# One conv moved behind the sixth tile, one moved ahead of a second stage, and two loads let loose singly

## The chip, the cores and the metric

The kernel runs on one core of a Trainium2 chip. The metric is the device time of one execution in microseconds (us), the median over several executions. Five engines work side by side and meet only at semaphores: TensorE (PE; its weight loads are shown as PEld), VectorE (DVE), ScalarE (ACT), GpSimd (POOL) and SyncE (SP), which here only issues transfers.

## The reference

The input `x` has 8 sequences of 4160 tokens with 192 channels. First comes a causal depthwise convolution of 7 taps whose weights are shared by the 24 channels of a head and normalised over the taps, then a feed-forward part whose hidden layer is the maximum of three products:

```python
w = exp(weight - max); w = w / sum(w)                 # [8 heads, 7 taps]
y[b, s, h, :] = sum_k w[h, k] * x_pad[b, s + k, h, :] # 33280 tokens in all
h = maximum(maximum(y @ w1, y @ w2), y @ w3)          # [tokens, 768]
out = h @ w_out                                       # [tokens, 192], float32
```

## The kernel before, in words

The 33280 tokens are 65 blocks of 512. Every block goes through the same stages.

**Convolution on TensorE.** The taps stand in a band matrix (`band`), and a matmul of a window of `x` with a slice of it gives convolved tokens. Blocks 0 to 3 use `conv_dense` (160 PE instructions: 80 matmuls of 32 columns and their weight loads). It writes channels by tokens into two PSUM tiles `D`, which ACT and DVE copy to `yd`; `cross` copies the two halves of the middle channels to each other. Blocks from 4 on use `conv` (64 matmuls and 64 loads): the result stands with tokens on the partitions in PSUM tiles `G`, `evac` (one ACT copy, one DVE copy for block 4) takes it to `ys`, `turn` issues two transposing DMAs from `ys` to `yp`, and `double` copies `yp` on POOL so that both halves of the partitions hold what they need.

**First stage, `l1(t, j)`.** For block `t` and hidden tile `j` of six: three pairs of matmuls of 512 columns, one lane on each half of the rows, with weights `w1-w3` (PSUM tile `lp`) and `w2-w3` (`lq`). `top` then makes `r = relu(lp)` on ACT and `h = max(r, lq)` on DVE. There are two buffers of `lp` (pool `psp`) and two of `lq` (pool `psq`), so tile `j+2` needs what ACT and DVE did with tile `j`.

**Second stage, `st2(t, upto)`.** 30 matmuls of 192 columns in each of two lanes give `out = h @ w_out + y @ (w3 @ w_out)`. They accumulate in tiles `po` of the pool `psw` (four buffers, which `D` and `G` also take). `upto` says how far each lane has come. At the half and at the end, `total` lets ACT copy one lane (`a`) and DVE add the other (`o`); both free a `po` buffer.

**Order.** The schedule is written by hand: each engine's queue holds the instructions as the program emits them. A loop over `t` from 2 on interleaves `l1(t, j)` with `st2(t - 1, ...)` and, now and then, a conv of a later block, the casts of `x` to fp16 on POOL (`cast_x`) and loads (`load_x`, on SP's queue). `meet` only empties the list of pending matmuls. Block 2 is the first turn of the loop. In it the kernel before emits: `l1(2, 0)`; the rest of block 0's second stage, `st2(0, (30, 30))`; `st2(1, (5, 5))`; `l1(2, 1)`; `conv_dense(3)` into two buffers of `psw`; then `st2` and `l1` in turn, with `conv(4)` after `l1(2, 3)`. Blocks 7, 8 and 9 are loaded into the fp32 buffers `xf_0`, `xf_1` and `xf_2` that blocks 0, 1 and 2 leave. Before each load, rows 32 to 63 of the buffer have to be set to zero (`zero_x`, by ACT for `xf_0`, by DVE for the others). The two transposing DMAs of `turn(4)` stand on SP between the loads of block 8 and those of block 9.

Of the kernel before, what the change touches and what calls it, by code (L numbers as in the profile page):

```python
# [28 lines left out]
def kernel(  # L29
# [12 lines left out]
    nc = tc.nc  # L42
# [45 lines left out]
    NQ = len(chunks_of[0])  # L88
    TOK = 32
    NR = NBLK // TOK // 2  # L90
# [6 lines left out]
        return rows  # L97

    const = ctx.enter_context(tc.tile_pool(name="const", bufs=1))
    x16p = ctx.enter_context(tc.tile_pool(name="x16p", bufs=2))  # L100
    x16q = ctx.enter_context(tc.tile_pool(name="x16q", bufs=2))
    ysp = ctx.enter_context(tc.tile_pool(name="ysp", bufs=2))
    ydp = ctx.enter_context(tc.tile_pool(name="ydp", bufs=4))
# [24 lines left out]
    def zero_x(t, q0=0, q1=NR, eng=None):  # L128

        if t >= NDENSE:  # L130
            get_x(t)
        xf = xbuf[t]
        if eng is not None:
            eng.memset(xf[TOK:HALF, q0:q1, :], 0.0)
            return
        zero = idle[TOK:HALF, 0:D]
        nc.scalar.copy(out=xf[TOK:HALF, q0:q1, :],
                       in_=bass.AP(tensor=zero.tensor, offset=zero.offset,
                                   ap=[list(zero.ap[0]), [0, q1 - q0], [1, D]]))
# [37 lines left out]
    def place(t):  # L177
        return pairs.get(t, (t, 0, 0))
# [3 lines left out]
    def cast_x(t):  # L182
        if not 0 <= t < NB:
            return
        xf, p0, _ = xin.pop(t)
        t0, u, nu = place(t)
        if u == 0:
            pool = x16q if nu == 4 else x16p
            x16s[t0] = pool.tile([P, NHEAD, 4, nu, 2, GRP], FP16, tag="x16", name=f"x16_{t0}")
        if p0:  # L190
            nc.gpsimd.memset(xf[0:p0, 0, :], 0.0)
        K = HALF + KR
        for r in range(2):
            nc.gpsimd.tensor_copy(out=x16s[t0][0:K, :, :, u, r, :].rearrange("p h j c -> p j h c"),  # L194
                                  in_=xf[0:K, 4 * r:4 * r + 4, :].rearrange("p j (h c) -> p j h c", c=GRP))
# [174 lines left out]
    def conv_dense(t, copies, pools=((None, None),) * 2, order=(0, 1)):  # L370


        yd = dense[t] = ydp.tile([P, NC, NBLK], FP16, tag="yd", name=f"yd_{t}")
        for n in order:
            slots_ = ((0, 1, 2, 3), (4, 5, 4, 5))[n]
            pool, tag = pools[n]
            ps = (pool or psw).tile([P, NBLK], FP32, tag=tag or "w", name=f"D{n}_{t}")
            for (q, b, row_lo, rlen, lo, hi, cc) in chunks_of[t]:
                for v in range(2):
                    for g, s in enumerate(slots_):  # L380
                        h = (32 * s + 31 * v) // GRP
                        nc.tensor.matmul(  # L382
                            ps[32 * g:32 * g + 32, lo:hi],
                            lhsT=xz[t][v][0:rlen, q, 32 * s:32 * s + 32],
                            rhs=band[0:rlen, h, cc:cc + hi - lo],
                            start=(v == 0), stop=(v == 1), tile_position=(0, 32 * g))
            copies[n](out=yd[:, 2 * n, :], in_=ps[:])
# [152 lines left out]
    def st2(t, upto):  # L540

        if t < 0:
            return
        if t not in halves:
            todo = [[], []]
            for s in range(4):
                for i in range(2):
                    row = slice(HALF * i, HALF * (i + 1))  # L550
                    m = [(-1, i)]
                    if s % 2 == i:
                        m.append((-1, 2))
                    hh = [(j, row) for j in range(NJ)]
                    m = hh + m if t == 0 else m + hh
                    todo[i] += [(s, n == 0, n == len(m) - 1, e) for n, e in enumerate(m)]
            if t == 0:

                todo = [[(n, first and n % 2 == 0, last, e)
                         for m in (False, True) for n, first, last, e in lane if (e[0] < 0) == m] for lane in todo]  # L560
            halves[t] = (todo, {}, [0, 0], {})
        todo, ps, at, ends = halves[t]

        def product(i, e):
            s, first, last, (j, c) = todo[i][e]
            b0 = s - s % 2
            row = slice(HALF * i, HALF * (i + 1))
            if (b0, i) not in ps:
                ps[b0, i] = psw.tile([P, 2, D], FP32, tag="w", name=f"po{i}_{t}_{s}")
            if j < 0:  # L570
                a, b = y_tok(t, i, c, s), m16[row, c // 2, :]
            else:
                assert done[t] > j
                a, b = hs[t][row, j, P * s:P * (s + 1)], wo[row, j, :]
            nc.tensor.matmul(ps[b0, i][:, s % 2, :], lhsT=a, rhs=b, start=first,  # L575
                             stop=last and (t > 0 or s % 2 == 1))

        def total(s):
            if t not in outs:
                outs[t] = outp.tile([P, 4, D], FP32, tag="o", name=f"o_{t}")  # L580
            a = tp.tile([P, 2, D], FP32, tag="a", name=f"a_{t}_{s}")
            nc.scalar.copy(out=a[:], in_=ps[s - 1, 0][:])  # L582
            nc.vector.tensor_add(out=outs[t][:, s - 1:s + 1, :], in0=a[:], in1=ps[s - 1, 1][:])  # L583

        while any(at[i] < upto[i] for i in range(2)):
            i = 0 if at[0] < upto[0] and (at[0] <= at[1] or at[1] >= upto[1]) else 1
            e = at[i]
            mm(i, D, lambda i=i, e=e: product(i, e))
            at[i] += 1
            s, _, last, _ = todo[i][e]  # L590
            if last:
                ends[s] = ends.get(s, 0) + 1
                if ends[s] == 2 and s % 2:
                    op(lambda s=s: total(s))
        emit()
# [57 lines left out]
    PQ = ((psp, "p"), (psq, "q"))  # L653
    WW = ((psw, "w"), (psw, "w"))
    WPWQ = ((psw, "w"), (psp, "p"), (psw, "w"), (psq, "q"))
    ACT, DVE = nc.scalar.copy, nc.vector.tensor_copy
# [45 lines left out]
    st2(0, (24, 24))  # L702
    meet()
    zero_x(0, NQ)
    zero_x(2, NQ, NR, nc.vector)
    zero_x(3, NQ, NR, nc.vector)
    load_x(7)
    cast_x(5)
# [20 lines left out]
    for t in range(2, NB):  # L729
        u = convs_at.get(t, NB)  # L730
        late = t > 2 and u < NB
        if t in (3, 4):
            double(t + 1)
        if t > 3:
            for v in range(casts.get(t - 1, 8) + 1, casts[t] + 1):
                cast_x(v)
        l1(t, 0)
        if t == 2:
            st2(0, (30, 30))
        elif t == 3:  # L740
            cast_x(8)
            nc.gpsimd.tensor_copy(out=m16[0:HALF, 2, :], in_=m16[HALF:P, 0, :])
            nc.gpsimd.tensor_copy(out=m16[HALF:P, 2, :], in_=m16[HALF:P, 1, :])
        if t > 3 and not late:
            op(lambda t=t: (store(t - 2, 0, 4, (nc.sync,)),
                            turn(t + 2, (2,)) if place(t + 2)[1:] == (0, 4) else None, load_on(t)))
        else:
            op(lambda t=t: store(t - 2, 0, 4, (nc.sync,)))
        cuts = ROOM if late else EVEN
        st2(t - 1, (cuts[0], cuts[0]))  # L750
        for j in range(1, NJ):
            l1(t, j)
            if late and j == 1:
                st2(t - 1, (cuts[0] + OWN + AHEAD, cuts[0] + OWN))
                meet()
                quad, second = u >= QUADS, u < QUADS or t == u - 3
                conv(u, WPWQ, range(4 * second, 4 * second + 4) if quad else range(NHEAD))
                for i in (0, 2):
                    evac(u, i)
                for i in (1, 3):  # L760
                    evac(u, i, nc.vector.tensor_copy)
                if second:
                    turn(u)
                load_on(t)
            if t == 2 and j == 1:
                meet()
                conv_dense(3, (ACT, DVE))
                zero_x(1, NQ, NR, nc.vector)
                cross(3, GP)
                load_x(8)  # L770
                cast_x(6)
            elif t == 2 and j == 3:
                meet()
                conv(u, WW)
                evac(u, 0)
                evac(u, 1, nc.vector.tensor_copy)
                turn(4)
                load_x(9)
                cast_x(7)
            st2(t - 1, (cuts[j], cuts[j]))  # L780
            if j == 1 and t > 4 and t + 2 in pairs and pairs[t + 2][1] % 2 == 0:
                double(t + 2)
            if t == NB - 1 and j == 3:
                op(lambda: store(NB - 2, 0, 2, (nc.sync,)))
        if t == NB - 1:
            op(lambda: store(NB - 2, 2, 4, (nc.sync,)))
# [29 lines left out]
```

## Time and profile before

| | |
|---|---|
| median of 4 runs | 455.27 us (454.81 to 455.78) |
| the profiled execution | 455.38 us, of which the span is 453.6 us |
| PE, PEld busy | 447.8 and 411.6 us |
| DVE, ACT, POOL busy | 358.7, 319.8 and 203.1 us |
| DMA | 72.03 MB, mean 159 GB/s |

The span begins with the first instruction and ends with the last; 1.8 us of the execution lie around it. Line numbers such as L507 are lines of the kernel before. A row of the timeline gives the start, the time, the engine, the line, the operation and, in brackets, the idle time of the engine before it with what ended it. "issue" stands where the engine waited for nothing that the profile shows. SPq rows are the issues of transfers on SP's queue, not the transfers.

### The profile page before, as it was taken

To read this page: it belongs to the slowest core of one execution; us is meant where nothing else is said; L and a number is where in the kernel's file an instruction comes from. 1 tells how busy PE (TensorE), PEld (TensorE's weight loads), DVE (VectorE), ACT (ScalarE), POOL (GpSimd) and SP (SyncE) were. 2 spreads that over 40 slices of the span, in tenths; PEclk is the share of its full clock that TensorE was granted. 3 is DMA by queue.
4 is the path that set the end of the run, shared out by engine and by line. 5 is a ranking of instruction groups with operands and counts; after the bars stand their busy time and mean duration, and the time that the engine had idled before them with its cause. 6 is when DMAs were issued, how large, how long until landed. Compare 5 with 4: busy or idle time off the path is not lost.

```text
span 453.6 us, 18554 instructions
## 1 busy us (share of the span) xinstructions
PE 447.8 (99%) x7730; PEld 411.6 (91%) x7730; DVE 358.7 (79%) x616; ACT 319.8 (70%) x605; POOL 203.1 (45%) x228
## 2 busy tenths in 40 slices
PE   8989999999999999999999999999999999999997
PEld 4468999999999999999999998899999999999996
DVE  7777787878888787888878778887878778787775
ACT  7767777767777677777767777777767777676664
POOL 2684926557453524635244454435346452505000
PEclk9999999999999999999999999999999999999999
DMA  7978997596985759687495949858596865734223
GB/s 204 218 186 148 219 178 218 147 207 167 159 198 140 172 132 180 160 174 195 115 194 135 215 111 178 191 130 189 128 173 162 186 178 117 122 86 106 59 72 106
DMA packets 127987, 72.03 MB, mean 159 GB/s; under 512 B 52064, under 2 KB 127711, under 8 KB 127903
## 3 DMA queue, kind: packets, MB, share of 16 engines
q1 hardware_dynamic: 127743, 70.75, 68.7%
q8 instruction: 60, 0.98, 1.0%
q14 instruction: 24, 0.20, 0.2%
q10 hardware_dynamic: 160, 0.10, 0.1%
HBM read 33.28 MB, written 25.56 MB: 130 GB/s over the span
## 4 chain that ended last, share of the span: by engine, by line
PE 95%; SPq 2%; DMA 1%; issue 0%; POOL 0%; DVE 0%; ACT 0%; POOLq 0%; DVEq 0%
PE po L575 36%; PE lq L507 31%; PE lp L507 22%; PE G L361 3%; DMA ws<-in_moe_w_dram 1%; PE lw L530 1%; SPq L227 1%; SPq L223 1%; PE D L382 0%; PE po L606 0%; PE lp L530 0%; SPq L164 0%; DVE h L495 0%; PE pm L341 0%; POOL xz L211 0%
## 5 line engine op out<-in xcount | busy, mean ns | idle before, releaser
L575 PE MATMUL po<-wo,h 64*128 64x192 f16 x3072 | 333.5, 243 | 0.0
L495 DVE TENSOR_TENSOR h<-r,lq 128x512 f16<-128x512 f16 x384 | 263.0, 686 | 85.4 <-ACT r L494 76.5
L494 ACT ACTIVATE r<-lp 128x512 f16<-128x512 f32 x384 | 229.0, 597 | 115.3 <-PE lp L507 100.9
L507 PE MATMUL lp<-yp,wd 64*128 64x512 f16 x1098 | 295.7, 376 | 0.0
L507 PE MATMUL lq<-yp,wd 64*128 64x512 f16 x1098 | 295.5, 376 | 0.0
L575 PEld LDWEIGHTS <-h 64*128 64x128 f16 x3072 | 243.0, 94 | 6.5 <-issue 4.3
L507 PEld LDWEIGHTS <-wd 64*128 64x128 f16 x2268 | 178.8, 94 | 12.2
L194 POOL CAST x<-xf 103x768 f16<-103x768 f32 x122 | 97.4, 827 | 110.6 <-DMA xf<-in_x_dram 87.9
L575 PE MATMUL po<-m,yp 64*128 64x192 f16 x720 | 141.0, 243 | 0.0
L424 POOL COPY yp<-yp 64x1536 f16<-64x1536 f16 (+1 forms) x62 | 89.6, 1445 | 90.7 <-DMA yp<-ys 82.7
L583 DVE TENSOR_TENSOR o<-a,po 128x384 f32<-128x384 f32 x128 | 70.0, 547 | 0.0
L575 PEld LDWEIGHTS <-yp 64*128 64x128 f16 x720 | 66.3, 94 | 0.4
L582 ACT COPY a<-po 128x384 f32<-128x384 f32 x128 | 60.4, 473 | 0.0
L401 ACT CAST ys<-G 128x384 f16<-128x384 f32 x61 | 26.3, 482 | 10.2 <-PE G L361 9.9
L401 DVE CAST ys<-G 128x384 f16<-128x384 f32 x61 | 31.0, 550 | 0.0
L361 PE MATMUL G<-x,band 39*32 39x192 f16 (+2 forms) x1152 | 17.5, 234 | 0.5 <-issue 0.5
L361 PEld LDWEIGHTS <-band 39*32 39x32 f16 x1152 | 10.7, 91 | 5.8 <-issue 5.3
L507 PE MATMUL lp<-yd,wd 64*128 64x512 f16 x36 | 9.7, 376 | 0.0
L507 PE MATMUL lq<-yd,wd 64*128 64x512 f16 x36 | 9.7, 376 | 0.0
L211 POOL CAST xz<-xf 112x160 f16<-112x160 f32 (+2 forms) x15 | 4.3, 335 | 9.6 <-DMA xf<-in_x_dram 8.1
L530 PEld LDWEIGHTS <-wd 128*128 128x128 f16 (+1 forms) x48 | 3.1, 98 | 6.0 <-issue 2.3
L382 PEld LDWEIGHTS <-xz 112*32 112x32 f16 x320 | 4.9, 108 | 2.9 <-POOL xz L211 1.2
(65 smaller groups left out, 94.7 us busy)
## 6 DMA issues: line engine op xcount, KB each, us to landing
xf<-in_x_dram SPq DMA_DIRECT2D x113, 234.0 KB
out_dram<-o SPq DMA_DIRECT2D x62, 384.0 KB
xf<-in_x_dram SPq DMA_DIRECT2D x7, 204.8 KB
xf<-in_x_dram SPq DMA_DIRECT2D x3, 420.0 KB
ws<-in_moe_w_dram SPq DMA_DIRECT2D x8, 128.0 KB
yp<-ys SPq DMA_TRANSPOSE x62
out_dram<-o SPq DMA_DIRECT2D x5, 192.0 KB
wos<-in_moe_w_out_dram SPq DMA_DIRECT2D x1, 576.0 KB
```

The source lines that it names most:

```text
L194: nc.gpsimd.tensor_copy(out=x16s[t0][0:K, :, :, u, r, :].rearrange("p h j c -> p j h c"), in_=xf[0:K, 4 * r:4 * r + 4, :].rearrange("p j ( ...
L361: nc.tensor.matmul(G[2 * (k // per) + i][TOK * j:TOK * (j + 1), k % per, :], lhsT=band[row, h, HALF * i + LAP:HALF * i + KR], rhs=x16s[t0] ...
L382: nc.tensor.matmul(ps[32 * g:32 * g + 32, lo:hi], lhsT=xz[t][v][0:rlen, q, 32 * s:32 * s + 32], rhs=band[0:rlen, h, cc:cc + hi - lo], star ...
L401: copy(out=slots[t][:, i % 2, :, :, GRP * h0:GRP * (h0 + per)].rearrange("p u r (h c) -> p h (u r) c", c=GRP), in_=G[i][:].rearrange("p h ...
L424: nc.gpsimd.tensor_copy(out=yp[HALF * i:HALF * (i + 1), 1, :, :, :, :].rearrange("p i u k n -> p (i u k n)"), in_=yp[HALF * (1 - i):HALF * ...
L494: nc.scalar.activation(out=r[:], in_=ps[0][:], func=AF.Relu)
L495: nc.vector.tensor_max(out=hs[t][:, j, :], in0=r[:], in1=ps[1][:])
L507: nc.tensor.matmul(ps[i][:], lhsT=w_of(i, c, j), rhs=y_all(t, i, c), start=(n == 0), stop=(n == NC - 1))
L530: nc.tensor.matmul(open_ps[t, j, i][:], lhsT=a, rhs=b, start=(t, j, i) not in begun, stop=(t, j, i) in begun)
L575: nc.tensor.matmul(ps[b0, i][:, s % 2, :], lhsT=a, rhs=b, start=first, stop=last and (t > 0 or s % 2 == 1))
L582: nc.scalar.copy(out=a[:], in_=ps[s - 1, 0][:])
L583: nc.vector.tensor_add(out=outs[t][:, s - 1:s + 1, :], in0=a[:], in1=ps[s - 1, 1][:])
```

## The change

In block 2's turn of the loop, and just ahead of it:

- `st2(1, (5, 5))` no longer stands behind `l1(2, 0)`. Its ten matmuls join the next ones, so that `st2(1, (10, 10))` comes as twenty behind `conv_dense(3)`.
- `conv_dense(3)` takes its two PSUM tiles from the pools of the first stage (`PQ`: one of `psp`, one of `psq`) where it took two of `psw`.
- `conv(4)`, with its copies and its two transposing DMAs, stands behind `l1(2, 5)` where it stood behind `l1(2, 3)`.
- The zeroing of `xf_1` and the loads of block 8 stand behind `l1(2, 2)` where they stood behind `l1(2, 1)`. The zeroing of `xf_2`, which stood ahead of block 2, stands behind `l1(2, 4)`, with the loads of block 9 right behind it. So on SP the loads of block 9 now stand ahead of the two transposing DMAs of `turn(4)`.
- The fp16 pool `x16p` has three buffers in place of two, because block 7 is now cast ahead of `conv(4)` in the program.

Every engine has the same instructions as before (15462 rows on PE, 612 on DVE, 605 on ACT, 137 on POOL, 190 on SP); their order differs.

```diff
-    x16p = ctx.enter_context(tc.tile_pool(name="x16p", bufs=2))
+    x16p = ctx.enter_context(tc.tile_pool(name="x16p", bufs=3))
...
     zero_x(0, NQ)
-    zero_x(2, NQ, NR, nc.vector)
     zero_x(3, NQ, NR, nc.vector)
     load_x(7)
     cast_x(5)
...
         cuts = ROOM if late else EVEN
-        st2(t - 1, (cuts[0], cuts[0]))
+        if t > 2:
+            st2(t - 1, (cuts[0], cuts[0]))
         for j in range(1, NJ):
             l1(t, j)
...
             if t == 2 and j == 1:
                 meet()
-                conv_dense(3, (ACT, DVE))
-                zero_x(1, NQ, NR, nc.vector)
+                conv_dense(3, (ACT, DVE), PQ)
                 cross(3, GP)
-                load_x(8)
                 cast_x(6)
-            elif t == 2 and j == 3:
+            elif t == 2 and j in (2, 4):
+                v = j // 2
+                zero_x(v, NQ, NR, nc.vector)
+                load_x(7 + v)
+                if j == 4:
+                    cast_x(7)
+            elif t == 2 and j == 5:
                 meet()
                 conv(u, WW)
                 evac(u, 0)
                 evac(u, 1, nc.vector.tensor_copy)
                 turn(4)
-                load_x(9)
-                cast_x(7)
             st2(t - 1, (cuts[j], cuts[j]))
```

## The prediction, made before the changed kernel was run

> **What bounds the kernel now.** I read the busy table first, then the chain, the windows of blocks 2, 3 and 4, and the timelines of PE, DVE, SP and POOL there.
>
> ```profile
> PE 447.8 (99%) x7730; PEld 411.6 (91%) x7730; DVE 358.7 (79%) x616; ACT 319.8 (70%) x605; POOL 203.1 (45%) x228
> PE 95%; SPq 2%; DMA 1%; issue 0%; POOL 0%; DVE 0%; ACT 0%; POOLq 0%; DVEq 0%
> q8 instruction: 60, 0.98, 1.0%
> ```
>
> TensorE is busy for 99% and makes 95% of the chain. A gap closed in it, or a new one, moves the end by as much, unless a later wait takes it back. The windows of block 2 (before its first `l1` to block 3's), block 3 and block 4 (us, PE, PEld, DVE, ACT, POOL):
>
> ```profile
> 24.89:35.33 10.44, 9.24 (x256) 6.28 (x254) 7.56 (x14) 5.64 (x12) 7.56 (x10) 1.00 0.72 171
> 35.33:42.47 7.14, 7.14 (x160) 6.53 (x158) 5.72 (x11) 5.10 (x11) 3.25 (x5) 1.00 0.68 144
> 42.47:49.60 7.13, 7.13 (x163) 6.70 (x161) 5.79 (x11) 5.17 (x11) 4.70 (x7) 1.00 1.13 191
> ```
>
> Block 3 costs what block 4 costs, so nothing is lost in it, and the clock is full. Block 2 loses time; PE's timeline shows where, and where block 4 starts:
>
> ```profile
> 25.54 0.66 PE L575 MATMUL po<-m,yd 64*128 64x192 f16 x12
> 26.75 0.64 PE L575 MATMUL po<-m,yd 64*128 64x192 f16 x3 [0.56 <-ACT a L582]
> ...
> 32.63 0.22 PE L361 MATMUL G<-x,band 39*32 39x48 f16 x9 [0.50 <-issue]
> ...
> 42.47 0.38 PE L507 MATMUL lp<-yp,wd 64*128 64x512 f16 x1
> ...
> 42.81 0.38 PE L507 MATMUL lq<-yp,wd 64*128 64x512 f16 x1
> ```
>
> And what block 4 needs: the loads and transposes on SP, the `double` on POOL.
>
> ```profile
> 30.98 0.78 SPq L164 DMA_DIRECT2D xf<-in_x_dram  x2
> 33.42 3.95 SPq L415 DMA_TRANSPOSE yp<-ys  x2
> 37.47 0.97 SPq L164 DMA_DIRECT2D xf<-in_x_dram  x2
> 38.53 0.41 SPq L647 DMA_DIRECT2D out_dram<-o  x1
> 39.09 4.03 SPq L415 DMA_TRANSPOSE yp<-ys  x2
> ...
> 39.05 1.71 POOL L424 COPY yp<-yp 64x768 f16<-64x768 f16 x2 [4.46 <-DMA yp<-ys]
> ...
> 45.73 2.99 POOL L424 COPY yp<-yp 64x1536 f16<-64x1536 f16 x2 [2.21 <-DMA yp<-ys]
> ```
>
> `turn(4)` starts on SP at 33.42, POOL sits 4.46 us until it has landed, and copies from 39.05 to 40.76. TensorE wants the second half of that copy at 42.81: 2.05 us to spare.
>
> **The change part by part.** The same instructions run, so the sum is one of waits. Clock: the profiled execution, 455.38 us, span 453.6; it lies 0.11 above the median of 455.27.
>
> *The early `st2(1)`.* The twelve matmuls at 25.54 take 0.042 each to issue (ten of them take 0.42 elsewhere, 34.02 to 34.44 in the chain), so PE is free at 26.04. The next ten need `po` buffers that ACT's two `a` copies (26.23 to 27.09) free. They end at 27.48 and need 0.42: 1.02 us of waiting, of which the row shows 0.56 whole. In the new order `l1(2, 1)` and `conv_dense(3)` stand there. `l1(2, 1)` starts at 26.04 (0.645 of issue). The conv starts 0.32 behind the last pair, as before, at 26.80. Its new buffers: the one in `psp` needs `r` of (2, 0), done at 26.33; the one in `psq` needs `h` of (2, 0), done at 27.05 and wanted at 27.32. Both in time. It ends at 27.83 (1.03), the twenty `st2` matmuls at 28.68 (0.85). Gain 1.02.
>
> *The 0.50 "issue" gap in `conv(4)`.* The code queue q8 moved 60 packets of 16 KB; PE ran 15460 instructions, 258 for each packet. I read the gap as code that came late: the 256 instructions ahead of it hold half of `conv_dense(3)` and most of `conv(4)` and ran in 3.1 us (29.0 to 32.1), where the average is 453.6/60 = 7.6. In the new order the same 256 take from 27.4 to 33.8, 6.4 us, so the gap should go: gain 0.50 (0 at the other end). The next 256 then run to the middle of the conv of block 5 in 3.8 us (33.8 to 37.6; 5.8 before): a gap of 0 to 0.5 may come back there. I take 0.
>
> ```profile
> 26.36 0.69 DVE L495 TENSOR_TENSOR h<-r,lq 128x512 f16<-128x512 f16 x1
> 30.42 0.54 DVE L134 MEMSET xf<- 32x576 f32 x1 [0.17 <-issue]
> 31.82 0.55 DVE L583 TENSOR_TENSOR o<-a,po 128x384 f32<-128x384 f32 x1
> ```
>
> *DVE's queue.* These three rows price a new wait. Zeroing `xf_1` now stands behind `h` of (2, 2), ahead of `o` and `h` of (2, 3). `l1(2, 2)` issues from 28.68; `r` starts when its last `lp` matmul ends, 29.52, `h` at 30.15. Then on DVE `h` 0.69, memset 0.18+0.54, `o` 0.55, `h` 0.69 with 0.08 of overlap at either end: `h` of (2, 3) ends at 32.74. `lq` of (2, 5) waits for it. PE is there at 31.95: 28.68, three `l1` of 0.645, three `st2` of 0.42, and 0.09 of wait for `h` of (2, 2). A new stall of 0.84. Before, `conv(4)` stood in between and covered it. If the memset overlapped fully the stall would be 0.1; I take 0.84, since both memset rows show the 0.17 ahead. The second memset (behind `h` of (2, 4)) delays `h` of (2, 5) and so the DVE copy of `ys`: 34.72 to 35.28. Block 3's first `po` waits for that copy: 0.05. Zeroing `xf_2` early was covered by the wait for `r`; leaving it out gains nothing.
>
> *Net in block 2.* `conv(4)` runs from 33.53 to 34.21, and block 3 starts at 34.63 instead of 35.33. After the 0.05 the lead is 0.65.
>
> *Where the lead goes: block 4.* Its conv comes 2.1 us of work later. The ACT copy of `ys` ends at 34.76 (33.40 before). SP must first issue block 9's loads, which wait for the memset of `xf_2` (34.07): 34.12 to 35.09. The transposes start at 35.15 instead of 33.42, 1.73 later, behind 479 KB of transfers. Landing, bounded by two rows: `turn(4)` before needed from 33.42 to about 38.56 (POOL's start at 39.05 less some 0.5 of its own), so 5.1 us: 40.3. The transposes of block 5 also stood right behind block 9's loads: from the start of those (37.47) to POOL's 45.73 it is 8.2 us, so 42.3; but they move twice the bytes, and a store of 393 KB ran with them. I take a third of the way, 40.95. Add 0.5 and the two copies, 1.71: `yp` of block 4 is whole at 43.2 (42.5 to 44.6 by the bounds). TensorE with its lead wants it at 42.16. So it waits 1.0 us, and `lq` of block 4 starts at 43.2 against 42.81: +0.4.
>
> [...]
>
> *Behind block 4* POOL zeroes and casts block 8, 1.97 us from the end of `double` (40.76 to 42.72). The conv of block 7 needs it 2.04 us behind `lq` (44.85 less 42.81), so it just holds: 0 to 0.2 more. Then `double(5)`, 3 us on POOL, ends near 49 with the first use near 50.3. The third `x16p` buffer takes a wait off POOL (0.34 us, not on the chain): 0. Blocks from 5 on keep their order.
>
> *Sum:* -1.02 -0.50 +0.09 +0.84 +0.05 makes -0.54 by the terms and -0.65 by the positions (0.1 that block 3 lost before on `lq`); the wait of about 1.0 for `yp` makes +0.4. 455.38 + 0.4 - 0.11 is 455.7 on the median.
>
> **The rivals.** One: the transposes come later still. For it: SP's row at 39.09 (8.2 us by the bound) and possible code packets on the same engines. From a landing at 41.5 on the loss is over 0.9; at the far bound it is 1.8, so 456.2 to 457.0. Against it: half the bytes, no store in the way. Two: the transposes are on time, by 39.9, and the lead of 0.65 stands: 454.6. For it: the row's 5.1 us hold a stretch from 35.3 to 36.9 in which DMA moves next to nothing. Three: DVE's new wait does not come either (the memset overlaps, or DVE gets its turns earlier), so conv and transposes are 0.8 earlier: -1.0 to -1.5, 453.8 to 454.3. Against it are the two memset rows. Four: the code gap comes back in block 5's conv: 0 to 0.5 off the lead, hidden wherever the wait for `yp` is the longer.
>
> **How the numbers follow.** The measurement tells about 0.2%, 0.9 us, from no change. The forecast case (lead used up, -0.3 to +1.0) has 0.42, of which 0.05 ends over 0.9. Rival one has 0.33, nearly all slower. Two, with four inside it, has 0.12, of which 0.05 is over 0.9 faster. Three has 0.13, all faster. Faster 0.19, same 0.43, slower 0.38. The range is 454.2 to 457.0: it leaves out most of three and the last of one. The likeliest case's own range is 455.0 to 456.3.
>
> **What would show it.** No 0.56 gap at `po` near 26, no 0.50 gap in `conv(4)`. A wait of `lq` (2, 5) for DVE `h` of about 0.8. Block 3 starting near 34.6. On SP, block 9's loads ahead of the transposes, these near 35.2. POOL's `double` starting at 41 to 42, and a gap in PE ahead of the first `lq` of block 4, released by POOL `yp`. If that gap is missing, the forecast is too slow by up to 1 us; if it is 2 us, rival one holds.

## The result, and the profile after

The changed kernel takes 456.9 us (median of 30 runs, 455.09 to 461.76). The kernel before takes 455.72 us (49 runs, 454.12 to 457.9). The ratio is 1.0035 [1.0023, 1.0048]: slower by some 0.35%, between 1.0 and 2.2 us. It was timed a second time, as `after_again`: 457.24 us, ratio 1.003 [1.001, 1.005]. Ten of the 30 runs are above 458 us, where none of the 49 of the kernel before beside them is (in the other sets it was 4 of 116).

Both profiled executions of the changed kernel were long ones (459.41 and 459.73 us), each for a reason of its own, so two are read side by side. First the windows of blocks 2, 3 and 4, cut as for the kernel before (us, PE, PEld, DVE, ACT, POOL; then the clock, the DMA share and GB/s). The first profile after:

```profile
24.12:37.75 13.63, 10.88 (x257) 7.46 (x254) 7.43 (x13) 5.64 (x12) 7.40 (x10) 0.87 0.55 130
37.75:46.08 8.33, 7.34 (x160) 6.18 (x157) 6.64 (x12) 5.86 (x12) 0.83 (x1) 1.00 0.93 176
46.08:53.77 7.69, 7.39 (x160) 6.59 (x161) 5.21 (x10) 4.34 (x9) 7.27 (x10) 1.00 0.71 166
```

And the second:

```profile
28.10:37.73 9.63, 9.08 (x257) 6.37 (x254) 6.96 (x13) 5.49 (x12) 6.03 (x9) 1.00 0.54 139
37.73:46.40 8.67, 7.44 (x161) 6.18 (x157) 6.67 (x12) 5.96 (x12) 0.82 (x1) 1.00 1.13 174
46.40:54.09 7.69, 7.40 (x161) 6.60 (x162) 5.18 (x9) 4.35 (x9) 7.28 (x10) 1.00 0.79 168
```

Before, the three blocks took 10.44, 7.14 and 7.15 us, 24.73 together. In the second profile they take 25.99, which is 1.26 more: block 2 gains 0.81, block 3 loses 1.53, block 4 loses 0.54. These 1.26 lie inside the interval that the ratio gives for the medians (1.0 to 2.2); that they are the typical loss can't be shown by one profile. (This execution is long because it reaches block 2 only at 28.10; it ran at half clock for 3.4 us from 23.5 on, ahead of it.) In the first profile block 2 alone takes 13.63. PE's timeline of that profile shows the two stories in one:

```profile
26.01 0.78 PE L382 MATMUL D<-band,xz 112*32 112x103 f16 x49
28.98 0.88 PE L382 MATMUL D<-band,xz 112*32 112x103 f16 x31 [2.20 <-issue]
...
35.99 0.37 PE L507 MATMUL lq<-yd,wd 64*128 64x512 f16 x1 [0.55 <-DVE h L495]
...
46.08 0.37 PE L507 MATMUL lp<-yp,wd 64*128 64x512 f16 x1 [0.99 <-POOL yp L424]
...
46.96 0.37 PE L507 MATMUL lq<-yp,wd 64*128 64x512 f16 x1 [0.29 <-POOL yp L424]
```

The wait at `po` (0.56 whole, 1.02 in all) and the gap in `conv(4)` are gone, as forecast. The three last rows are in both profiles, 35.97, 46.40 and 47.28 in the second:

```profile
35.97 0.37 PE L507 MATMUL lq<-yd,wd 64*128 64x512 f16 x1 [0.55 <-DVE h L495]
...
46.40 0.37 PE L507 MATMUL lp<-yp,wd 64*128 64x512 f16 x1 [1.14 <-POOL yp L424]
...
47.28 0.37 PE L507 MATMUL lq<-yp,wd 64*128 64x512 f16 x1 [0.29 <-POOL yp L424]
```

The row of 2.20 is in the first alone: TensorE stopped behind the 49th matmul of `conv_dense(3)` and waited for nothing that the profile shows. What followed it is seen in the column of the clock, the third from the right, of the same profile's windows:

```profile
28.00:29.00 1.00, 0.02 (x4) 0.01 (x4) 0.00 (x0) 0.00 (x0) 0.88 (x3) 0.99 1.06 246
29.00:30.00 1.00, 1.00 (x35) 0.84 (x36) 0.10 (x1) 0.00 (x0) 1.00 (x2) 0.50 0.96 273
...
31.00:32.00 1.00, 1.00 (x12) 0.63 (x10) 0.00 (x0) 0.00 (x0) 1.00 (x2) 0.50 0.00 0
32.00:33.00 1.00, 1.00 (x16) 0.62 (x14) 0.00 (x0) 0.28 (x1) 0.10 (x1) 0.80 0.00 0
```

The clock fell to a half for 3.4 us (three windows at 0.50 and 0.4 of the next). Half of 3.4 is 1.7, and with the 2.20 that makes 3.9 of the 4.0 by which block 2 is longer here than in the second profile. So a loss of about 1.25 has to be explained, and beside it a gap that some executions have.

The wait for `h` has the cause that the prediction named. DVE's timeline of the first profile shows the memset and its 0.17 between `h` of (2, 2), which ends at 34.04, and `o`:

```profile
34.22 0.54 DVE L134 MEMSET xf<- 32x576 f32 x1 [0.17 <-issue]
34.78 0.56 DVE L583 TENSOR_TENSOR o<-a,po 128x384 f32<-128x384 f32 x1
35.26 1.28 DVE L495 TENSOR_TENSOR h<-r,lq 128x512 f16<-128x512 f16 x2
```

For the wait for `yp`, SP's and POOL's timelines of the second profile:

```profile
31.74 6.32 SPq L164 DMA_DIRECT2D xf<-in_x_dram  x5
38.15 2.98 SPq L415 DMA_TRANSPOSE yp<-ys  x2
...
45.52 1.70 POOL L424 COPY yp<-yp 64x768 f16<-64x768 f16 x2 [9.64 <-DMA yp<-ys]
```

From the issue at 38.15 to the copies at 45.52 it is 7.4 us, where it was 5.6 before. The semaphore events of the trace give more. Each transpose lands in 16 parts. Fifteen parts of the later one landed from 43.32 to 43.44, the sixteenth at 45.02. Meanwhile a 16 KB packet of the code queue moved, from 42.68 to 43.84: it began 0.64 ahead of the first of the fifteen. The DMA view of that stretch has it as:

```profile
q8 instruction: 1, 0.02, 6.2%
```

6.2% of 16 engines for 1.16 us is 1.15 us of one engine: the packet held a single engine nearly all that time. That this engine is the one that carried the sixteenth part is inferred; the trace does not name it. In the first profile it is the same: fifteen landings from 43.01 to 43.15, the last at 44.70, a code packet from 42.40 to 43.60.

### The profile page after: what moved, and what is told of

Read it like the earlier page. It is cut to its first block, busy times and chain, and to the rows that moved or that the text cites. A ratio compares the mean times of both kernels' runs of the same rounds, so it can differ in the third digit from the quotient of the medians.

```text
span 457.6 us, 18555 instructions
## 1 busy us (share of the span) xinstructions
PE 448.6 (98%) x7730; PEld 413.2 (90%) x7730; DVE 358.2 (78%) x616; ACT 319.7 (70%) x605; POOL 203.3 (44%) x228
## 4 chain that ended last, share of the span: by engine, by line
PE 95%; DMA 2%; SPq 1%; issue 1%; DVE 0%; POOL 0%; ACT 0%; DVEq 0%; POOLq 0%
PE po L575 36%; PE lq L507 31%; PE lp L507 22%; PE G L361 3%; PE lw L530 1%; DMA xf<-in_x_dram 1%; PE D L382 1%; DMA yp<-ys 1%; PE lp L530 1%; PE po L606 0%; SPq L227 0%; SPq L223 0%; PE pm L341 0%; PE lq L530 0%; SPq L164 0%
## 5 line engine op out<-in xcount | busy, mean ns | idle before, releaser
L382 PE MATMUL D<-band,xz 112*32 112x103 f16 (+1 forms) x320 | 6.0, 236 | 3.1 <-issue 2.2
```

Of the source, the lines that this page charges most:

```text
L382: nc.tensor.matmul(ps[32 * g:32 * g + 32, lo:hi], lhsT=xz[t][v][0:rlen, q, 32 * s:32 * s + 32], rhs=band[0:rlen, h, cc:cc + hi - lo], star ...
```

## The experiments

The table gives PE's time for blocks 2, 3 and 4 (from the first matmul of block 2 to the first of block 5) in each profiled execution, and the medians. "Start" is the first matmul of block 2. Each ratio is to the kernel before timed in the same set (medians of 455.41 to 455.73).

| kernel | start | block 2 | block 3 | block 4 | sum against before | median us | ratio to before |
|---|---|---|---|---|---|---|---|
| before | 24.89 | 10.44 | 7.14 | 7.15 | | 455.72 | |
| after | 24.12 | 13.63 | 8.33 | 7.69 | +4.92 | 456.9 | 1.0035 [1.0023, 1.0048] |
| after_again | 28.10 | 9.63 | 8.67 | 7.69 | +1.26 | 457.24 | 1.003 [1.001, 1.005] |
| e1_early | 25.55 | 9.23 | 7.14 | 7.15 | -1.21 | 455.52 | 0.9998 [0.9981, 1.0016] |
| e1_look2 | 24.51 | 10.51 | 7.14 | 7.15 | +0.07 | 454.71 | 0.9977 [0.9961, 0.9994] |
| e12_early3 | 24.26 | 10.85 | 7.15 | 7.14 | +0.41 | 454.16 | 0.9975 [0.9953, 0.9997] |
| e2_late | 25.17 | 10.72 | 8.27 | 7.69 | +1.95 | 457.34 | 1.0045 [1.0018, 1.0072] |
| e3_turn_first | 24.58 | 10.39 | 7.66 | 7.69 | +1.01 | 456.57 | 1.0022 [1.0005, 1.0039] |
| e4_shift | 25.60 | 9.74 | 8.64 | 7.69 | +1.34 | 457.32 (one run) | |
| e5_shift128 | 25.57 | 11.21 | 7.25 | 7.69 | +1.42 | 460.86 | 1.0095 [1.0064, 1.0126] |
| e6_zero_early | 26.95 | 9.49 | 12.93 | 7.15 | +4.84 | 457.73 | 1.0025 [0.9995, 1.0055] |
| e7_l1_first | 25.12 | 10.70 | 7.14 | 7.15 | +0.26 | 455.81 | 0.9991 [0.9966, 1.0015] |
| e8_light | 25.63 | 8.90 | 8.44 | 7.69 | +0.30 | 457.12 | 1.0035 [1.0018, 1.0052] |
| e9_conv_late | 25.08 | 10.23 | 7.26 | 7.14 | -0.10 | 455.59 | 0.9999 [0.9972, 1.0026] |
| e10_both | 26.84 | 8.79 | 7.26 | 7.15 | -1.53 | 455.18 | 0.9994 [0.9975, 1.0012] |
| e11_loads | 24.95 | 10.08 | 7.41 | 7.15 | -0.09 | 455.83 | 0.9997 [0.9978, 1.0015] |

In each profile the span differs from that before by the difference of the start and this sum, within 0.15 us. Three lose more behind block 4: `e3_turn_first` 0.7 and `e8_light` 0.5 in block 5 (7.07 and 6.86, where before takes 6.36), and `e5_shift128` 3.7 (below). So the start of block 2, which varies by up to 4 us, hides what these blocks gain or lose in a single execution.

### The two halves of the change

`e1_early` is the kernel before with the early part alone:

```diff
-        st2(t - 1, (cuts[0], cuts[0]))
+        if t > 2:
+            st2(t - 1, (cuts[0], cuts[0]))
...
-                conv_dense(3, (ACT, DVE))
+                conv_dense(3, (ACT, DVE), PQ)
```

> The early part alone: the first ten st2 matmuls of block 1 go behind conv_dense(3), which takes its PSUM from psp and psq; conv(4) and the loads of blocks 8 and 9 stay where they were before. Theory C (code arrives late): the gap of the changed kernel, 2.2 us in the middle of conv_dense(3) after 49 of its 80 matmuls, is there again at the same matmul, 0.5 to 2.5 us long, with the granted clock at 0.5 for some 3 us behind it where the gap is over 2 us; block 4's first lq does not wait for yp; time +0.0 to +0.4% against before. Theory T (the late conv(4) makes the loss, through yp): no such gap or a gap that costs nothing at the end, time 0.1 to 0.3% below before (the 1.02 us wait at po gone). Theory B (the gap is a wait for the psq buffer): the gap stands at the 41st matmul, where the second D tile begins.

`e2_late` is the changed kernel with these lines put back, so that only the late part is left.

> The late part alone: conv(4) behind l1(2, 5), loads of blocks 8 and 9 let loose singly ahead of turn(4), x16p with three buffers; the early st2 and conv_dense(3) as before. Theory C: no gap of over 0.3 us in conv_dense(3), because the 1.02 us wait at po is back in front of it and the code has arrived; the granted clock stays at 1.0. Both theories: block 4's first lq waits 1 to 3 us for yp, since conv(4) is some 2 us later and block 9's loads go first. Theory T: time +0.3 to +0.6%, as the whole change or worse. Theory C with T adding: +0.1 to +0.4%.

The late part alone is slower, by as much as the whole change. The early part alone is not: its profile gains 1.21 in block 2 and loses nothing behind it. So the loss comes from the late part. In `e2_late` PE waits for the same three things as after, 0.55, 0.59 and 0.29 in its rows, beside the wait at `po` (0.56) that it keeps and a gap in the conv of block 5 (39.08, below).

### The transposes ahead of block 9's loads

`e3_turn_first` is the changed kernel with the loads of block 9 behind `turn(4)`:

```diff
-                load_x(7 + v)
+                if j == 2:
+                    load_x(8)
...
                 turn(4)
+                load_x(9)
```

> The changed kernel with block 9's loads issued behind the two transposes of turn(4), all else as changed. Theory T: the transposes land 1 to 2 us sooner after conv(4), the wait of block 4's first lq (1.28 us in the changed kernel) shrinks to under 0.5 us, and the time falls by 0.2 to 0.4% against the changed kernel, to within 0.2% of before. Theory C: the gap in conv_dense(3) stays, with it most of the loss; the time falls by under 0.2% against the changed kernel and stays above before.

It does not undo the loss: 1.0022, with an interval that overlaps that of the whole change, so the times can't tell how much it takes off. The transposes still began 10.6 us behind the start of block 2, and fifteen parts of the later one were down at 39.18, 4.0 us after the issue at 35.20. But the last came at 41.25. A code packet moved from 38.74 to 40.02. PE's timeline:

```profile
42.63 0.37 PE L507 MATMUL lp<-yp,wd 64*128 64x512 f16 x1 [0.33 <-ACT r L494]
...
43.51 0.37 PE L507 MATMUL lq<-yp,wd 64*128 64x512 f16 x1 [0.29 <-POOL yp L424]
```

With the loads ahead (`after_again`) the fifteen parts took 5.29 us from the issue, so the loads cost 1.3 us of landing in these two profiles. The last 2.07 us here come with the code packet.

### Moving the code packet

By the row of q8 in the kernel before (60 packets, 0.98 MB) a code packet has 16 KB, and the 15462 instructions of PE make 258 for each; 256 is an estimate from that. If so, instructions put in at the very start move every boundary by as many. `e4_shift` puts 20 tiny matmuls (40 PE instructions with their weight loads) into the warm-up of the changed kernel, `e5_shift128` 64 (128 instructions):

```diff
     keep_warm(5, psp, "p")
+    pad = psp.tile([P, NBLK], FP32, tag="p", name="pad")
+    for _ in range(20):
+        nc.tensor.matmul(pad[:, 0:8], lhsT=idle[:, 0:P], rhs=idle[:, 0:8], start=True, stop=True)
```

> The changed kernel with 20 tiny matmuls (8 columns, 40 PE instructions with their weight loads) added to the warm-up at the start, while TensorE waits for its first data. Theory C: the gap in conv_dense(3) moves 20 matmuls forward, from after 49 of its 80 to after 29, because the boundary between two 256-instruction blocks of code moves by 40 instructions. Theory B, or any other wait tied to what conv_dense(3) does: the gap stays after the 49th or stands at the 41st.

> The changed kernel with 64 tiny matmuls (128 PE instructions) added to the warm-up, so that every boundary of 256 instructions stands 128 instructions earlier in the work. In four looks (the changed kernel, the late part alone, transposes first, shift by 40) one of the 16 landings of turn(4)'s second transpose came 1.5 to 2.1 us behind the other fifteen, while a 16 KB code packet, called for by the conv of block 5, ran. Theory K (that code packet holds up one DMA engine and with it the last landing): the boundary now falls ahead of the conv of block 5, the packet runs 1 to 2 us sooner, the last landing comes under 0.5 us behind the others, and the wait of block 4's first lq falls from 0.9 to 1.3 us to under 0.4 us. Rival X (block 9's loads ahead of it are what holds up the landing): the last landing is 1.5 to 2 us late as before. A gap in conv_dense(3) may show elsewhere or not at all.

The gap in block 5's conv shows the boundary. Without the shift it comes with 19 of the conv's 64 matmuls left, in `e2_late`, with the 40 instructions put in ahead of it with 39 left, in `e4_shift`. That is 20 matmuls sooner, as it must be. (In `conv_dense(3)`, where the shifted gap was expected, this profile has none.) PE's timeline of `e2_late`:

```profile
39.08 0.31 PE L361 MATMUL G<-x,band 39*32 39x96 f16 x19 [0.24 <-issue]
```

and of `e4_shift`:

```profile
38.61 0.54 PE L364 MATMUL G<-x,band 39*32 39x96 f16 x39 [0.53 <-issue]
```

The sixteen profiles have fourteen such gaps of over 0.2 us between 20 and 60 us. With PE's matmuls and weight loads counted in order of start, from 0, every one ends at number 961, 1217 or 1473, which stand 256 apart, and the last code packet ended 1.3 to 1.7 us ahead of that. So these "issue" gaps inside runs of small matmuls are read as code that had not come, 256 instructions of PE with each packet; the shift agrees.

This also tells which packet meets the transposes. It is not the code that the conv of block 5 waits for: that moved before (36.05 to 37.61 in `e2_late`). It is the next one. In the eight profiles that have the conv of block 4 late and number 1473 in the conv of block 5 it began 1.0 to 1.9 us after number 1473 had started.

In `e4_shift` the late landing stays (fifteen by 41.07, the last at 42.60, a code packet from 40.35 to 41.57). In `e5_shift128` the packet moves from 37.70 to 39.12, just behind the issue of the transposes (37.21) and long before they land, and all sixteen parts land from 42.51 to 42.65: the straggler is gone. This is the test of the code packet as the cause of the late sixteenth part, and it held. Blocks 3 and 4 lose 0.65 together, where they lose 2.07 in `after_again`. The kernel before agrees: a packet moved from 34.78 to 36.05 while its transposes were under way, and all parts of the later one landed from 38.35 to 38.54. In these profiles the later transpose had a late part only where a packet was running when the first of its parts landed. The kernel as a whole got slower, 1.0095. Its profile shows a different reason; the timeline of PE has

```profile
77.60 0.25 PE L578 MATMUL po<-wo,h 64*128 64x192 f16 x1 [1.94 <-issue]
```

a gap of 1.94, which ends at number 3009, eight times 256 behind 961, and half the clock for 3.4 us behind it, beside one of 1.36 in block 2. All four runs of it are above 458.5 us.

### The zeroing

`e6_zero_early` is the changed kernel with both memsets of DVE ahead of block 2:

```diff
+    zero_x(1, NQ, NR, nc.vector)
+    zero_x(2, NQ, NR, nc.vector)
     zero_x(3, NQ, NR, nc.vector)
...
-                zero_x(v, NQ, NR, nc.vector)
```

> The changed kernel with both zeroings (xf_1, xf_2) on DVE ahead of block 2; the loads of blocks 8 and 9 stand in the same places of SP's queue but wait for no memset. Theory D (DVE's queue, the step of the prediction): the wait of lq of (2, 5) for DVE h, 0.85 us in the looks so far, falls under 0.15 us, conv(4) starts 0.7 to 0.8 us sooner against the start of l1(2, 0), block 9's loads are issued some 5 us sooner, the transposes start as soon as ys is copied, about 1 us sooner. If the wait for yp then still ends block 4's start, most of it is lost again: time 0.1 to 0.3% below the changed kernel, still not below before. If the memsets cost nothing, the time is that of the changed kernel.

The wait of `lq` of (2, 5) for `h` is gone, and all parts of the transposes land together (42.30 to 42.43). The profiled execution is the longest of its twelve, 462.19 us. It reaches block 2 at 26.95, 2.1 later than before, and most of the rest comes from one row on PE's timeline:

```profile
42.16 0.43 PE L361 MATMUL G<-x,band 39*32 39x96 f16 x19 [2.70 <-issue]
```

The same boundary as in `e2_late`, but 2.70 us late, with 6.8 us at half clock from 41.4 on. The median, 457.73 with an interval that takes in no change, can't say what the memset is worth. The wait that it causes is shown; its price on the median is not.

### Another place for `conv_dense(3)`

`e7_l1_first` is `e1_early` with `conv_dense(3)` and what follows it behind `l1(2, 2)`:

```diff
-            if t == 2 and j == 1:
+            if t == 2 and j == 2:
...
-            st2(t - 1, (cuts[j], cuts[j]))
+            if t > 2 or j > 1:
+                st2(t - 1, (cuts[j], cuts[j]))
```

> The early part alone, with l1(2, 2) put ahead of conv_dense(3) as well and no second stage of block 1 before it; conv(4) and the loads where they were before. Theory C (the code for the middle of conv_dense(3) comes at its own time): six long matmuls use 0.65 us and only 12 instructions, so conv_dense(3) starts 0.7 to 1.2 us later than in the early part alone and the code has arrived: no gap over 0.3 us there, yet the 1.02 us wait at po is not there either. Time 0.1 to 0.3% below before. If the early part's gain is lost elsewhere (not to code), the time is that of before, as for the early part alone.

No difference: 0.9991. The gap stands in `conv(4)` with nine matmuls left, where the kernel before has it, now 0.72, and block 2 takes 10.70.

### Less traffic ahead of block 2

`e8_light` is `e1_early` with the loads of blocks 6 and 7 held back until the load of block 8:

```diff
-    for t in range(NDENSE, XBUF):
+    for t in range(NDENSE, XBUF - 1):
         load_x(t)
...
-    load_x(7)
     cast_x(5)
...
+                load_x(6)
+                load_x(7)
                 load_x(8)
                 cast_x(6)
```

> The early part alone, with the loads of blocks 6 and 7 issued behind the store of block 0 (about 28 us) instead of ahead of it (20 to 26 us), so that less stands on the DMA engines when the code for the middle of conv_dense(3) is wanted. Theory C with traffic: the code packet that ran at 25.8 to 27.1 us runs 1 to 2 us sooner, no gap in conv_dense(3) in the look, the gain of 1.0 to 1.2 us stands in most executions: ratio 0.997 to 0.999. If the later loads push turn(4) and the casts past their need, block 4 or the conv of block 5 waits 0.5 to 2 us and the ratio is over 1. If traffic does not matter, it is that of the early part alone, 1.000.

Slower, by 0.35% against before and more against the early part alone. Its block 2 is the second shortest of all (8.90), and the code packet ahead of its conv started at 24.12, in `e1_early` at 25.20, so less traffic there may have helped. But the loads now stand on SP right ahead of `turn(4)`:

```profile
29.26 4.05 SPq L164 DMA_DIRECT2D xf<-in_x_dram  x7
33.41 3.66 SPq L415 DMA_TRANSPOSE yp<-ys  x2
```

The transposes start early, 33.41, and land at 41.58, 8.2 us later and all parts together; the one code packet in that time ran from 35.37 to 36.59, long before. Block 3 then loses 1.30, of which a code gap of 0.72 in the conv of block 5 is a part, and the first `lq` of block 4 waits another 0.29 for `yp`. So in this profile, meant for something else, loads ahead of the transposes are enough to make them late.

### The late conv and the loads, one without the other

`e9_conv_late` is the kernel before with `conv(4)`, its copies and its transposes moved, and the third buffer of `x16p`. Block 9's loads and the cast of block 7 stand in the same branch and move with them, so block 9's loads stay behind `turn(4)`; zeroing and the other loads stay. `e10_both` is the same with the early part as well. `e11_loads` is the changed kernel with `conv(4)` back behind the fourth tile.

```diff
# e9_conv_late, against before; e10_both, against e1_early
-            elif t == 2 and j == 3:
+            elif t == 2 and j == 5:
# e11_loads, against after
-            elif t == 2 and j == 5:
+            elif t == 2 and j == 3:
```

> The kernel before with conv(4), its copies and turn(4) behind l1(2, 5) alone (and the third x16p buffer); the loads stand as before, block 8's behind l1(2, 1), block 9's behind turn(4), with both memsets where they were. Theory L (the lateness of turn(4) makes the loss; the loads ahead of it add): the wait of lq (2, 5) for DVE h is under 0.2 us, the transposes start 10.0 to 10.6 us behind l1(2, 0) (8.5 before), the last landing is late by 1.5 to 2 us where the code packet of block 5's conv meets it, and block 4's first lq starts 18.2 to 19.0 us behind l1(2, 0) (17.92 before, 19.87 in the late part alone): ratio 1.000 to 1.003, under the 1.0045 of the late part alone. If the loads made the whole loss, the ratio is 0.998 to 1.000.

> The kernel before with both moves of work but none of the loads: the early part, and the conv of block 4 behind the sixth tile with its two transposes ahead of the loads of block 9. Theory (the late conv is harmless by itself, the loads and the zeroing cost): no wait of lq (2, 5) for h, transposes landed some 14.2 us behind the start of l1(2, 0) and POOL's double at about 14.8 unless a code packet runs with the landing, block 4 starts 0.5 to 1.2 earlier than before: 454.3 to 455.6. Rival (conv so late plus the shifted code boundary costs in itself): a gap in conv_dense(3) or block 5's conv of 0.5 to 2 us, or the landing 1.5 late: 456.3 to 457.5.

> The changed kernel with the conv of block 4 put back behind the fourth tile; early part, zeroing and loads let loose one by one as in the changed kernel. Theory (the loads cost because they stand ahead of the late transposes; DVE's memset costs because nothing on TensorE covers it): the transposes of block 4 stand between the loads of blocks 8 and 9 again and the conv covers the memset, so 454.3 to 455.6 and no wait for yp. Rival (loads let loose one by one cost in themselves, by the memset in DVE's queue): a wait of 0.5 to 0.85 for h of (2, 3) or (2, 4) and 456.0 to 456.8.

None of the three is slower: 0.9999, 0.9994, 0.9997. Neither the late conv nor the loads let loose one by one cost anything that these intervals (some 0.2% to either side) tell; together (`e2_late`, and the changed kernel) they do. (`e11_loads`, at 455.83, lies between what its two theories gave. It has no wait for `h` and none for `yp`, but the gap in `conv(4)` is 0.84.) In `e9_conv_late` the transposes start even later than in the changed kernel, 10.46 us behind the start of block 2 against 10.05. Its timelines of SP and POOL:

```profile
35.53 2.64 SPq L415 DMA_TRANSPOSE yp<-ys  x2
38.27 0.97 SPq L164 DMA_DIRECT2D xf<-in_x_dram  x2
...
39.83 1.70 POOL L424 COPY yp<-yp 64x768 f16<-64x768 f16 x2 [5.14 <-DMA yp<-ys]
```

They land 3.79 us after the issue, at 39.32, and POOL begins 14.75 us behind the start of block 2, where it begins at 17.42 in the second profile after. So the late transposes would have been in time. In `e10_both` it is the same (35.86 to 39.60, 3.74 us). Luck is in it: the code packet behind block 5's conv began at 39.81 and 39.55 there, 0.5 behind the last landing and just as it came, where in `e3_turn_first` it began 0.27 ahead of the first. In `e10_both` TensorE is busy without a break in blocks 2 and 3:

```profile
26.84:35.63 8.79, 8.79 (x256) 6.44 (x254) 7.33 (x14) 5.62 (x12) 7.49 (x10) 1.00 0.60 158
35.63:42.89 7.26, 7.26 (x161) 6.18 (x158) 5.88 (x11) 5.05 (x11) 2.60 (x4) 1.00 0.54 122
```

Four kernels, each with the stretch from the issue of the transposes to their last landing, show what goes with it. The DMA views of these stretches, `e10_both` (35.86 to 39.60) first:

```profile
DMA packets 833, 0.21 MB, mean 57 GB/s; under 512 B 832, under 2 KB 832, under 8 KB 832
```

before (33.40 to 38.55):

```profile
DMA packets 1063, 0.39 MB, mean 75 GB/s; under 512 B 845, under 2 KB 1061, under 8 KB 1061
```

`after_again` (38.15 to 45.02):

```profile
DMA packets 2529, 1.24 MB, mean 180 GB/s; under 512 B 1380, under 2 KB 2527, under 8 KB 2527
```

`e8_light` (33.40 to 41.60):

```profile
DMA packets 2448, 1.40 MB, mean 171 GB/s; under 512 B 909, under 2 KB 2446, under 8 KB 2446
```

The transposes themselves are 0.20 MB, all there is in the first but for one code packet. With 0.21, 0.39, 1.24 and 1.40 MB moved in the stretch, it lasts 3.74, 5.15, 6.87 and 8.2 us. The order is that of the bytes, and 1.58 of the 6.87 are the late part's. A longer stretch also takes in more of what was issued behind the transposes, so the order alone does not prove the cause; the loads moved ahead and behind (`e8_light`, `e3_turn_first`) are the better evidence.

### Again: the changed kernel, and the early part

> The changed kernel once more, on the same chip as the three above and with another profiled execution. Theory C: the gap in conv_dense(3), if it shows, stands after the 49th matmul again, of another length, with a half clock behind it only where it is over 2 us; the timed executions spread over several us, and the upper ones are those with the long gap. The wait of lq of (2, 5) and that for yp are there in every look.

> The early part alone once more, for a second profiled execution and twelve more times. In the first look block 4's first lq started 16.70 us behind l1(2, 0) instead of 17.92, with no gap in conv_dense(3), yet the median was that of before. Theory C: some executions have the code gap in conv_dense(3) behind the 49th matmul and lose there what the others gain; this look may show it, and the times spread wider than those of before. Rival: the gain of 1.2 us is real in all executions and the median was off by chance; then the ratio comes out under 0.9985.

> The early part alone a third time, beside the two others. Theory (it closes 1.02 us of waiting at po and loses nothing): 454.4 to 455.2, ratio 0.997 to 0.999. Rival (the gain is taken back later, as the first set's 0.9998 says): 455.3 to 455.7.

The changed kernel's loss came again. The early part alone was timed three times: 0.9998, 0.9977, 0.9975. Two of the three intervals lie below 1. It is the best version found, some 0.2% under the kernel before, though the first set does not show it. Its profiles can say why the gain varies. `e1_early` had no gap in block 2 and gained 1.21. `e12_early3` had two gaps on PE's timeline, the first at the place of the 2.20 above, the second at that of the kernel before:

```profile
28.14 0.54 PE L382 MATMUL D<-band,xz 112*32 112x103 f16 x31 [1.23 <-issue]
...
32.42 0.22 PE L361 MATMUL G<-x,band 39*32 39x48 f16 x9 [0.57 <-issue]
```

`e1_look2` had 0.64 and 0.57 there. The wait at `po` that the early part takes out had given the code time to come: in the kernel before, number 961 started at 28.71, 1.59 behind the end of its code packet (27.12), and the gaps end 1.3 to 1.7 behind theirs. Without the wait, the code is on time in some executions only.

## Why the prediction was wrong

The forecast was 455.7 us, 0.4 above before, with no measurable change likeliest. The time is 456.9, 1.2 above the 455.72 measured beside it. The slower side won, at the landing that rival one gave and by the second of its two reasons, a code packet. Point by point, with all places counted from the first matmul of block 2 and the second profile after as the measure:

- **The wait at `po`, a gain of 1.02:** right. It is gone in every kernel with the early part, and in `e1_early`, which has no gap, block 2 is 1.21 shorter.
- **The stall of 0.84 for `h`:** right. `lq` of (2, 5) starts 0.93 behind `lp` at 35.04, where 0.10 is usual, so 0.83.
- **Block 2 and the lead:** right within 0.16 in this profile. The lead was forecast as 0.65 and is 0.81. That it has no code gap is chance: in the first profile block 2 is 3.19 longer than before.
- **The transposes' start:** right. Forecast 10.26, measured 10.05.
- **"I take a third of the way, 40.95":** this is the step that failed. Counted as above that landing is 16.06, with `yp` whole at 18.3. Measured are 16.92 for the last part and 19.12 for `yp`. Of the difference of 0.86 in the landing all is the one late part: the other fifteen were down at 15.34, sooner than forecast and just sooner than the near bound of 40.3 (15.41). The prediction had the landing as a question of bytes in front, and took a value between two rows for that. The code packet stands in it as a half-sentence of rival one ("possible code packets on the same engines"), without a place or a price. Its place could be read off the trace of before, where the packet behind the boundary in block 5's conv began at 39.88, 1.83 after number 1473, and the prediction had that boundary at 37.6: by this the packet begins at an estimated 39.4 and may still run when the parts land, from 40.3 on. Its price was not to be had from that trace, in which the later transpose has no late part.
- **The sum:** forecast +0.4 for the start of `lq` of block 4. With 19.17 against 17.92 it is +1.25, which is the forecast plus what the landing was late. Rival one had it at over 0.9 for a landing from 41.5 on; on that axis the last part landed at 41.81.
- **Behind block 4, "0 to 0.2 more":** right. Blocks 5 and 6 take 6.36 and 7.14 us, as before.
- **The code gap, "I take 0":** wrong in many executions. The prediction looked at the boundary in `conv(4)`, which did get time, and at the one in block 5's conv. It used the boundary ahead of both, in `conv_dense(3)`, as the start of a stretch (27.4) and did not ask whether the code for it had come. The early part brings that boundary forward and takes away its cover, the wait at `po`. The trace of before had a price: its packet ended at 27.12, and the code in `conv(4)` could run 1.30 after its own, so 28.4 at the soonest where the prediction had 27.4, an estimated gap of 1.0, as much as the gain. Gaps there were 2.20 in the first profile after, 0.44 in `e3_turn_first`, 0 in the second. The one of 2.20 cost 1.7 by the clock as well. The long runs (ten of 30 above 458) fit that, but only profiled executions show a gap, so this link is argued.
- **Rival two, the transposes on time:** is what `e10_both` shows, which has both moves of work and keeps zeroing and loads in their old order: 3.74 us from issue to landing, the blocks 1.53 shorter. With the zeroing let loose and block 9's loads behind the transposes (`e3_turn_first`) fifteen parts were on time and one was not.
- **The chances:** the parts add up to 0.18 faster and 0.44 same, where the text has 0.19 and 0.43. Nothing rests on it.

Open stays why `e10_both`, 1.53 shorter in these blocks, is timed at only 0.9994. Its profiled execution came to block 2 at 26.84, 1.95 later than before. The starts in the table run from 24.12 to 28.10, and the changed kernel alone gave both ends, so one profile can't tell chance from cause. How much of the 1.26 falls to the memset, the loads and the code packet each is not settled on the medians either: the pieces are worth 0.83, about 1.1 (fifteen parts down at 15.34 against 14.24 in `e9_conv_late`) and 1.5 at their places, they overlap, and one hides another.

## What to carry to other kernels

When a step that ends in a transfer is moved later, ask two things of the landing: how many bytes its queue has let loose ahead of it, and whether a code packet moves at that time. In these profiles the code boundaries stood 256 instructions of TensorE apart (numbers 961, 1217 and 1473). Counted on from a gap that the profile calls "issue", that gives the other boundaries, and those that a change moves into a stretch of small matmuls, or takes the cover from, may show. Put loads that are wanted late behind the transfer that is wanted soon, not ahead of it: fifteen parts took 5.29 us from the issue with the loads ahead (`after_again`) and 4.0 with them behind (`e3_turn_first`). Here `e10_both`, with zeroing and loads in their old order, is no slower than before, and the changed kernel is. Block 9's loads by themselves did not make that difference: in `e3_turn_first` they stand behind, and the code packet met the landing.

## What the runs showed of the hardware

- A code packet of 16 KB was running when the first of the sixteen parts of `turn(4)`'s later transpose landed, and one part came 1.5 to 2.1 us behind the others (1.55, 1.53, 2.07, 1.53 and 1.58 in the profiles of after, `e2_late`, `e3_turn_first`, `e4_shift` and `after_again`). POOL's copy began 0.50 us behind that last part (44.70 and 45.20 in the first profile after, 45.02 and 45.52 in the second). In `e5_shift128`, where the packet had ended 3.4 us ahead of the first landing, there is none. The earlier transpose of the two does not go by this: in the first profile after, all its parts landed from 42.68 to 42.83 with the packet running since 42.40, and in the kernel before two came at 37.81 and 38.07, behind fourteen from 37.30 to 37.42, though the packet had ended at 36.05.
- The same code boundary (number 1473) cost anything from 0 (`e9_conv_late`) to 2.70 us (`e6_zero_early`) in executions of nearly the same program. Wherever it cost something, the code ran 1.3 to 1.7 us behind the end of its packet.
- With gaps of 1.94 (`e5_shift128`), 2.20 (after) and 2.70 us (`e6_zero_early`) TensorE fell to half clock for 3.4, 3.4 and 6.8 us; with gaps of 1.36 (`e5_shift128`) and 1.23 (`e12_early3`) it did not (clock 1.00 in the windows around them). In `after_again` it fell for 3.4 us without one long gap, at 23.5, when PE had been idle for 1.0 of the 3 us from 20 to 23. So no run shows an idle time from which the clock falls: the "over 2 us" of two expectations was the author's estimate from the one gap of 2.20, and 1.94 was enough.
